# Scale of V in a windowed-attention and gated-MLP kernel: row sums transposed by a transfer instead of by TensorE

## The chip, the cores and the metric

The kernel runs on one core of a Trainium2 chip. The metric is the device time of one execution in microseconds (us); the kernel before has a median of 650.21 us in 3 runs (648.14 to 650.54). The engines are named as in the profile: PE (TensorE; its weight loads are listed apart as PEld), DVE (VectorE), ACT (ScalarE), POOL (GpSimd) and SP (SyncE, which issues the DMA transfers of this kernel). Each takes its instructions in order.

## The reference

Eight batches, each with 8 heads of 576 positions and 64 channels: attention with a window of 128 positions and a linear bias, then a gated MLP over the joined heads.

```python
scores = scale * np.matmul(q, k.transpose(0, 1, 3, 2))
mask = (rel >= 0) & (rel < window)                 # window = 128
scores = np.where(mask, scores + bias[None], -1000000000.0)
attn = np.exp(scores - np.max(scores, axis=-1, keepdims=True))
attn = attn / (np.sum(attn, axis=-1, keepdims=True) + 1e-09)
x = np.matmul(attn, v)                             # heads joined: (8, 576, 512)
...
h = np.maximum(x @ w_in, 0.0)                      # 512 -> 1024
u, v = (h[..., :d_ff // 2], h[..., d_ff // 2:])
v_n = (v - mu) / np.sqrt(var + 1e-06)
v_s = np.einsum('ts,bsd->btd', w_spatial, v_n) + b_spatial[None, :, None]
return ((u * v_s) @ w_out).astype(np.float32)
```

## The kernel before

Work is built from a planner. Each step is put in with `plan.add(engine, weight, due, f, reads, writes)`: an engine, an estimate of its time, a due time, and the parts of buffers that it reads and writes. `plan.order()` then walks through a modelled time and lets each engine take, of the steps whose inputs are there, the one that is due first; `plan.either` lets the engine that would be done first (ACT or DVE) have a step. The resulting order is what each engine's queue holds. A changed weight or a step left out can so move other steps, on every engine.

Attention goes by pairs of heads, 4 pairs in each of 8 batches. The first five pairs go another way (`raw_tile`). The other 27 go through `attention`, once each, and one such pass is called a unit here. In a unit, in the numbers of the lines of the kernel before:

- L409 and L411 load Q and K (`qkraw`) and V (`vraw`), three buffers each. L520 makes the scores on PE in two groups, into PSUM banks `s` (4 of them).
- L531 adds bias and mask and takes the maximum (DVE), L537 exponentiates and sums (ACT), L545 and L549 make the reciprocals (DVE).
- L557 (ACT) and L562 (DVE) write the scaled probabilities as two float16 parts, high and low, into `pq0` and `pq1`. L568 transposes each by one DMA transfer inside SBUF into `pt` (18 blocks of 128 columns).
- V is split in float16 parts as well, `vh` and `vl`, which needs a power of two that fits the largest V of the unit. L579 (ACT) takes absolute values and sums each of the 128 rows into `am`; the values go to `vl`, which is only scratch at that time. The largest of the 128 row sums, which lie on 128 partitions, is found with the help of PE: L583 transposes the column into one row of a PSUM bank `x`, L587 and L588 (DVE) take the maximum and clamp it as bfloat16, L593 spreads it to all partitions by two products with constant rows `ones` (2^-12 and 2^-13/4096), and L599 and L600 (DVE) keep the exponent bits: the scale for V in `am` column 5, the one for the result in column 6.
- L604 (DVE) or L607 (ACT) writes `vh`, L611 (DVE) `vl`. L624 multiplies probabilities and V on PE into two banks `x` (2 of them), L633 (ACT) and L637 (DVE) write the result's two parts to `xt`, half by half.

The MLP of a batch goes by units of 8 to 14 products into PSUM banks `m` (2 of them): L689 and L711 (columns that are normalised, 4 groups and 1 group), L741 (`u`), L762 (the product along the positions), L788 (output `o`, copied out of the bank at L267 by ACT or DVE and stored by L798). PE's queue interleaves the MLP of one batch with the attention of the next. The seam between two batches is where the last L788 of one is followed by the first L689 of the next, which needs `xt` of all four units.

Of the kernel before, what the change touches and what calls it, by code (L numbers as in the profile page):

```python
# [9 lines left out]
F32 = mybir.dt.float32  # L10
F32R = mybir.dt.float32r
BF16 = mybir.dt.bfloat16
# [126 lines left out]
def attn_gmlp_kernel(ctx, tc, qk, v, w_in, w_spT, b_sp, w_out, outT):  # L139
# [3 lines left out]
    nc = tc.nc  # L143
# [31 lines left out]
    def fixed(shape, dtype, name):  # L175
        t = const.tile(shape, dtype, name=name)
        return Buf(lambda: t)

    def dve(n, fast=False):
        return 75 + n / (1.92 if fast else 0.96)  # L180
# [13 lines left out]

    nhalf = fixed([P, 1], F32, "nhalf")
    ident = fixed([P, P], F32, "ident")
    ones = fixed([1, 2 * P], BF16, "ones")
    tabs = [fixed([P, 2 * P], BF16, f"tab{h}") for h in range(H)]
    win = fixed([P, NC_, 2, DF], F32R, "win")
    wout = fixed([P, ND, 2, DM], F32R, "wout")  # L200
# [23 lines left out]
    def constants():  # L224
        def f():
            nc.gpsimd.iota(relf(), [[-1, 2 * P]], base=P, channel_multiplier=1, allow_small_or_imprecise_dtypes=True)
        plan.add("POOL", 400, 0, f, (), [(relf, 0)])

        def f():
            nc.vector.memset(maskt(), 0.0)  # L230
        plan.add("DVE", dve(256), 0, f, (), [(maskt, 0)])

        def f():
            nc.gpsimd.affine_select(maskt(), maskt(), [[-1, 2 * P]], ALU.is_ge, MASKED, base=P, channel_multiplier=1)
            nc.gpsimd.affine_select(maskt(), maskt(), [[1, 2 * P]], ALU.is_ge, MASKED, base=-1, channel_multiplier=-1)
        plan.add("POOL", 800, 1, f, [(maskt, 0)], [(maskt, 0)])

        def f():
            nc.vector.memset(ident(), 1.0)
            nc.vector.memset(ones()[:, :P], 2.0 ** -12)  # L240
            nc.vector.memset(ones()[:, P:], 2.0 ** -13 / PSC)
            nc.vector.memset(nhalf(), -0.5)
            nc.vector.memset(rstat(), 1.0)
        plan.add("DVE", dve(400), 500, f, (), [(ident, 0), (ones, 0), (nhalf, 0)] + [(rstat, k) for k in range(8)])

        def f():
            nc.gpsimd.affine_select(ident(), ident(), [[-1, P]], ALU.is_ge, 0.0, base=0, channel_multiplier=1)
            nc.gpsimd.affine_select(ident(), ident(), [[1, P]], ALU.is_ge, 0.0, base=0, channel_multiplier=-1)
        plan.add("POOL", 600, 500, f, [(ident, 0)], [(ident, 0)])

        def f():
            nc.vector.tensor_scalar(minus(), ident(), -1.0, None, ALU.mult)
        plan.add("DVE", 150, 501, f, [(ident, 0)], [(minus, 0)])
        for j in range(2):
            def f(j=j):
                nc.vector.memset(stat[j](), 1.0)
            plan.add("DVE", dve(64), 600, f, (), [(stat[j], x) for x in range(99)])
        for h in range(H):
            def f(h=h):
                slope = 2.0 ** (-8.0 * (h + 1) / H)  # L260
                nc.vector.scalar_tensor_tensor(tabs[h](), relf(), -8.0 * slope, maskt(), ALU.mult, ALU.add)
            plan.add("DVE", dve(256), 1000 + h * 4000, f, [(relf, 0), (maskt, 0)], [(tabs[h], 0)])
# [237 lines left out]
    def attention(b, p):  # L500
# [70 lines left out]

        vh, vl = (plan.buf(work, tag, 2, [P, NQ, P], F16) for tag in ("vh", "vl"))
        am = plan.buf(work, "am", 2, [P, 8], F32)
        one = plan.buf(work, "one", 2, [1, 2], BF16)
        mp = plan.buf(ps, "x", 2, [P, 512], F32)
        d = due - 3000

        def f():
            nc.scalar.activation(vl(), vr(), AF.Abs, accum_out=am()[:, 0:1])  # L579
        plan.add("ACT", act(NQ * P, 1), d, f, VRS, [(vl, 0), (am, 0)])  # L580

        def f():
            nc.tensor.transpose(mp()[0:1, 0:P], am()[:, 0:1], ident())  # L583
        plan.add("PE", SWITCH // 2, d + 1, f, [(am, 0), (ident, 0)], [(mp, 0)])

        def f():
            nc.vector.tensor_reduce(one()[:, 0:1], mp()[0:1, 0:P], AX.X, ALU.max)  # L587
            nc.vector.tensor_scalar(one()[:, 0:1], one()[:, 0:1], 2.0 ** -98, 2.0 ** 126, ALU.max, ALU.min)  # L588
        plan.add("DVE", 400, d + 2, f, [(mp, 0)], [(one, 0)])

        def f():
            for k in range(2):
                nc.tensor.matmul(mp()[:, P + k:P + k + 1], ones()[:, k * P:(k + 1) * P], one()[:, 0:1], start=True, stop=True,  # L593
                                 skip_group_check=True)
        plan.add("PE", SWITCH, d + 3, f, [(one, 0), (ones, 0)], [(mp, 1)])

        def f():
            bits = 0x7F800000
            nc.vector.tensor_scalar(am()[:, 5:7].bitcast(I32), mp()[:, P:P + 2].bitcast(I32), bits, None, ALU.bitwise_and)  # L599
            nc.vector.tensor_scalar(am()[:, 5:6].bitcast(I32), am()[:, 5:6].bitcast(I32), bits, None, ALU.bitwise_xor)  # L600
        plan.add("DVE", 150, d + 4, f, [(mp, 1)], [(am, 1)])

        def fv():
            nc.vector.tensor_scalar(vh(), vr(), am()[:, 5:6], None, ALU.mult)  # L604
# [4 lines left out]

        def f():  # L610
            nc.vector.scalar_tensor_tensor(vl(), vr(), am()[:, 5:6], vh(), ALU.mult, ALU.subtract)  # L611
        plan.add("DVE", dve(NQ * P) + 30, d + 6, f, VRS + [(am, 1), (vh, 0)], [(vl, 0)])

        xt = plan.buf(work, "xt", 6, [P, 2 * S + R], F32R)
        xps = [plan.buf(ps, "x", 2, [P, 512], F32) for _ in range(2)]
# [257 lines left out]
```

## Time and profile before

| | |
|---|---|
| Median of 3 runs | 650.21 us (648.14 to 650.54) |
| Profiled execution | 648.05 us, span 646.3 us, granted clock 0.992 |
| Busy of PE, PEld, DVE, ACT, POOL | 96%, 82%, 81%, 67%, 5% of the span |
| Transpose L583 | 27 times, 270 ns |
| Spreading products L593 | 54 times, 158 ns |
| Transfers L568 | 54, 4.7 us from issue to landing (median) |

The span is the profiled execution without what lies before its first and after its last instruction. A share of the span is a mean over the beginning (weights are prepared, raw pairs), some six equal batches, and an end without attention. In the windows and the timeline the first number is the start in us from the span's start, the second the time.

### The profile page before, as it was taken

The page shows a single profiled execution, that of the slowest core. Times are in us where ns is not written, and L with a number is a line of the kernel's source. Part 1 is how long each engine was busy: PE and PEld are TensorE (multiplying, and loading weights), DVE is VectorE, ACT ScalarE, POOL GpSimd, SP SyncE. Part 2 cuts the span into 40 slices and gives each one's busy share as a digit, 9 for nine tenths or more (in the row PEclk, how much of TensorE's full clock was granted, in tenths as well). Part 3 has the DMA queues.
Part 4 walks back from the last instruction along what each step waited for, and adds up shares of the span by engine and source line. Part 5 has one row for each costly group of instructions (what it writes and reads, how often), then busy time and mean ns, then how long its engine had stood idle before and what let it go on. Part 6 is the DMA issues. An engine that isn't in the chain of part 4 may idle for free.

```text
span 646.3 us, 14141 instructions
## 1 busy us (share of the span) xinstructions
PE 619.0 (96%) x5037; PEld 529.8 (82%) x5037; DVE 524.2 (81%) x1897; ACT 430.9 (67%) x1322; POOL 29.6 (5%) x53
## 2 busy tenths in 40 slices
PE   4879999999999999999999999999999999999997
PEld 2445688778899879988898979988898978988997
DVE  6999898999887979887887979887887979873632
ACT  4698675989585848686686848676686857662211
POOL 1000010000200010000100010000100010000100
PEclk9998799999999999999999999999999999999999
DMA  7903013799156863778165753858166751733001
GB/s 264 329 20 130 19 62 119 169 209 202 55 132 133 190 107 93 155 155 184 40 143 127 191 112 89 154 152 188 32 154 125 193 113 10 132 79 76 2 20 55
DMA packets 149291, 79.34 MB, mean 123 GB/s; under 512 B 128610, under 2 KB 139874, under 8 KB 149220
## 3 DMA queue, kind: packets, MB, share of 16 engines
q1 hardware_dynamic: 149220, 78.44, 51.8%
q8 instruction: 39, 0.64, 0.4%
q14 instruction: 32, 0.26, 0.1%
HBM read 37.13 MB, written 9.44 MB: 72 GB/s over the span
## 4 chain that ended last, share of the span: by engine, by line
PE 79%; DVE 17%; issue 1%; DMA 1%; ACT 1%; SPq 1%; ACTq 0%; DVEq 0%
PE m L762 16%; PE m L741 16%; PE m L788 14%; PE m L689 13%; PE s L520 8%; PE x L624 6%; DVE pq L562 4%; PE m L711 2%; DVE prob L436 2%; DVE prob L531 2%; DVE gs L298 1%; DMA pt<-in_qk_dram 1%; DVE prob L450 1%; DVE u L770 1%; DVE o L267 1%
## 5 line engine op out<-in xcount | busy, mean ns | idle before, releaser
L537 ACT ACTIVATE prob<-prob,stat 128x128 f32<-128x128 f32 (+1 forms) x270 | 125.4, 466 | 13.6 <-DVE stat L531 12.4
L762 PE MATMUL m<-wsp,vn 128*128 128x288 f32 x768 | 124.3, 299 | 0.7 <-DVE u L770 0.7
L788 PE MATMUL m<-gs,wout 128*128 128x288 f32 x768 | 113.5, 301 | 0.3 <-DVE gs L776 0.2
L762 PEld LDWEIGHTS m<-wsp,vn 128*128 128x128 f32 x768 | 107.5, 188 | 6.7 <-issue 1.9
L557 ACT ACTIVATE pq<-prob,stat 128x128 f16<-128x128 f32 x270 | 103.1, 464 | 12.7 <-ACT prob L537 10.2
L741 PE MATMUL m<-xt,win 128*128 128x288 f32 x768 | 111.6, 298 | 0.0
L788 PEld LDWEIGHTS m<-gs,wout 128*128 128x128 f32 x768 | 103.3, 188 | 7.2 <-issue 1.7
L562 DVE SCALAR_TENSOR_TENSOR pq<-prob,stat,pq 128x128 f16<-128x128 f32 x270 | 104.0, 437 | 4.3 <-ACT pq L557 3.7
L741 PEld LDWEIGHTS m<-xt,win 128*128 128x128 f32 x768 | 103.9, 188 | 4.1 <-issue 2.3
L689 PE MATMUL m<-win,xt 128*128 128x512 f32 x384 | 93.5, 396 | 1.7 <-DVE o L267 1.7
L531 DVE CUSTOM_DVE_ANT_0 prob<-s,tab 128x128 f32<-128x128 f32 (+1 forms) x270 | 89.2, 376 | 2.6 <-PE s L520 2.1
L689 PEld LDWEIGHTS m<-win,xt 128*128 128x128 f32 x384 | 71.5, 189 | 18.2 <-DVE o L267 2.8
L520 PE MATMUL s<-qkraw 64*128 64x256 f32 (+2 forms) x540 | 66.5, 360 | 1.5 <-DVE stat L531 1.3
L770 DVE TENSOR_TENSOR u<-m,u 128x288 f32<-128x288 f32 x64 | 28.9, 451 | 34.2 <-PE m L762 34.2
L520 PEld LDWEIGHTS s<-qkraw 64*128 64x128 f32 (+1 forms) x540 | 42.0, 175 | 16.2 <-issue 9.0
L659 POOL TENSOR_TENSOR st<-st,nhalf 128x1 f32<-128x1 f32 (+1 forms) x40 | 25.6, 640 | 560.4 <-DVE st L655 548.0
L537 ACT ACTIVATION_READ_ACCUMULATOR prob<-prob,stat 128x1 f32 x270 | 50.6, 187 | 0.0
L267 ACT COPY o<-m 128x288 f32<-128x288 f32 x37 | 14.6, 395 | 46.2 <-PE m L788 45.9
L624 PE MATMUL x<-pt,vh 128*64 128x256 f16 (+6 forms) x756 | 41.7, 229 | 0.0
L271 ACT ACTIVATE vt<-m 128x512 f32<-128x512 f32 x31 | 18.5, 598 | 33.0 <-DVE st L654 16.1
L637 DVE SCALAR_TENSOR_TENSOR xt<-x,am,xt 128x288 fp32r<-128x288 f32 x54 | 26.2, 507 | 17.1 <-ACT xt L633 17.0
L624 PEld LDWEIGHTS <-vh 128*64 128x64 f16 x756 | 31.7, 110 | 5.8 <-issue 3.5
(132 smaller groups left out, 820.7 us busy)
## 6 DMA issues: line engine op xcount, KB each, us to landing
qkraw<-in_qk_dram SPq DMA_DIRECT2D x28, 576.0 KB, 3.9
out_dram<-o SPq DMA_DIRECT2D x64, 144.0 KB, 2.0
vraw<-in_v_dram SPq DMA_DIRECT2D x28, 320.0 KB, 2.9
vn<-in_w_in_dram SPq DMA_DIRECT2D x6, 512.0 KB, 7.1
pt<-in_w_out_dram SPq DMA_DIRECT2D x4, 512.0 KB, 4.5
gs<-in_w_spT_dram SPq DMA_DIRECT2D x4, 288.0 KB, 5.0
xt<-in_w_in_dram SPq DMA_DIRECT2D x2, 512.0 KB, 6.8
qkraw<-in_qk_dram SPq DMA_DIRECT2D x3, 320.0 KB, 8.3
```

The costliest lines, as they stand in the source:

```text
L520: nc.tensor.matmul(sc[k][j]()[:m, i, :k1 - k0], raw()[rows, 0, t * P:t * P + m], raw()[rows, 1, k0:k1], start=True, stop=True)
L531: nc.vector.tensor_tensor_reduce(pt(), sc()[:m, i, :n], tabs[h]()[:m, c0:c0 + n], -0.125, 3e38, ALU.add, ALU.min, st()[:m, NM, j, t:t + 1])
L537: nc.scalar.activation(pt(), pt(), AF.Exp, bias=st()[:m, NM, j, t:t + 1], scale=-1.0, accum_out=st()[:m, SM, j, t:t + 1])
L557: nc.scalar.activation(pq[j]()[:m, 0, cs], prob[j]()[:m, cs], AF.Copy, scale=st()[:m, RC, j, t:t + 1])
L562: nc.vector.scalar_tensor_tensor(pq[j]()[:m, 1, cs], prob[j]()[:m, cs], st()[:m, RC, j, t:t + 1], pq[j]()[:m, 0, cs], ALU.mult, ALU.subtract)
L624: nc.tensor.matmul(xp()[j * D:(j + 1) * D, x0:x0 + n], l()[:, kt, j * D:(j + 1) * D], rhs[:, o:o + n], start=j not in seen, stop=False, sk ...
L637: nc.vector.scalar_tensor_tensor(xt()[:, S + R + hf * HS:S + R + (hf + 1) * HS], xp()[:, :HS], am()[:, 6:7], xt()[:, qs].bitcast(F32), ALU ...
L689: nc.tensor.matmul(pt(), xt[c]()[:, X0[a] + t * P:X0[a] + (t + 1) * P], win()[:, c, w, DH:DF], start=(n == 0), stop=(n == 3 * NC_ - 1))
L741: nc.tensor.matmul(pt()[:, :HS], win()[:, c, w, d * P:(d + 1) * P], xt[c]()[:, X0[a] + hf * HS:X0[a] + (hf + 1) * HS], start=(n == 0), sto ...
L762: nc.tensor.matmul(pt()[:, :HS], l, r, start=(n == 0), stop=(n == len(ops) - 1))
L770: nc.vector.tensor_tensor(u(), pt()[:, :HS], u(), ALU.mult)
L788: nc.tensor.matmul(pt()[:, :HS], wout()[:, d, w, e * P:(e + 1) * P], gs[d]()[:, a, :], start=(n == 0), stop=(n == 3 * ND - 1))
```

## The change

Per unit, the column of row sums is copied 128 times side by side as bfloat16 into the first of the five 128-column blocks of `vl` (`wide(0)`, new L584, on DVE), and one DMA transfer from SP transposes this 128x128 block inside SBUF into the second block (`wide(1)`, new L588). Every partition then holds all 128 sums, and DVE does the rest there in one step of five instructions: maximum (new L593), clamp (L594), exponent bits (L595), product with the two constants in `powers`, which takes the place of `ones` (L596), and the inversion of the exponent for the scale of V (L597). The three instructions on PE, their bank `x` and the bfloat16 buffer `one` go. The planner is told 300 for the transfer and 600 for the step on DVE. Lines behind it lose 3 in number: L624 becomes L621, L689 L686, L788 L785.

```diff
-        one = plan.buf(work, "one", 2, [1, 2], BF16)
-        mp = plan.buf(ps, "x", 2, [P, 512], F32)
...
         def f():
             nc.scalar.activation(vl(), vr(), AF.Abs, accum_out=am()[:, 0:1])
-        plan.add("ACT", act(NQ * P, 1), d, f, VRS, [(vl, 0), (am, 0)])
-
-        def f():
-            nc.tensor.transpose(mp()[0:1, 0:P], am()[:, 0:1], ident())
-        plan.add("PE", SWITCH // 2, d + 1, f, [(am, 0), (ident, 0)], [(mp, 0)])
-
-        def f():
-            nc.vector.tensor_reduce(one()[:, 0:1], mp()[0:1, 0:P], AX.X, ALU.max)
-            nc.vector.tensor_scalar(one()[:, 0:1], one()[:, 0:1], 2.0 ** -98, 2.0 ** 126, ALU.max, ALU.min)
-        plan.add("DVE", 400, d + 2, f, [(mp, 0)], [(one, 0)])
-
-        def f():
-            for k in range(2):
-                nc.tensor.matmul(mp()[:, P + k:P + k + 1], ones()[:, k * P:(k + 1) * P], one()[:, 0:1], start=True, stop=True,
-                                 skip_group_check=True)
-        plan.add("PE", SWITCH, d + 3, f, [(one, 0), (ones, 0)], [(mp, 1)])
+        plan.add("ACT", act(NQ * P, 1), d, f, VRS, [(vl, 0), (vl, 1), (am, 0)])
+
+        wide = lambda k: vl()[:, k, :].bitcast(BF16)
+
+        def f():
+            nc.vector.tensor_copy(wide(0), am()[:, 0:1].to_broadcast([P, P]))
+        plan.add("DVE", dve(P), d + 1, f, [(am, 0)], [(vl, 0)])
+
+        def f():
+            nc.sync.dma_start_transpose(out=wide(1), in_=wide(0))
+        plan.add("SP", 300, d + 2, f, [(vl, 0)], [(vl, 1)])
 
         def f():
             bits = 0x7F800000
-            nc.vector.tensor_scalar(am()[:, 5:7].bitcast(I32), mp()[:, P:P + 2].bitcast(I32), bits, None, ALU.bitwise_and)
+            nc.vector.tensor_reduce(am()[:, 1:2], wide(1), AX.X, ALU.max)
+            nc.vector.tensor_scalar(am()[:, 2:3], am()[:, 1:2], 2.0 ** -98, 2.0 ** 126, ALU.max, ALU.min)
+            nc.vector.tensor_scalar(am()[:, 2:3].bitcast(I32), am()[:, 2:3].bitcast(I32), bits, None, ALU.bitwise_and)
+            nc.vector.tensor_scalar(am()[:, 5:7], powers(), am()[:, 2:3], None, ALU.mult)
             nc.vector.tensor_scalar(am()[:, 5:6].bitcast(I32), am()[:, 5:6].bitcast(I32), bits, None, ALU.bitwise_xor)
-        plan.add("DVE", 150, d + 4, f, [(mp, 1)], [(am, 1)])
+        plan.add("DVE", 600, d + 4, f, [(vl, 0), (vl, 1), (powers, 0)], [(am, 1)])
```

What this does to the order, at three places of a steady batch. First PE in the middle of a batch, between two output units (`m<-gs,wout`) and the product along the positions (`m<-wsp,vn`); the last two rows of the piece of before come twice there.

```order
L788 MATMUL m<-gs,wout 128x288 x12
L583 MATMUL x<-ident,am 1x128
L520 MATMUL s<-qkraw 64x192 x2
L788 MATMUL m<-gs,wout 128x288 x12
L593 LDWEIGHTS ones
L593 MATMUL x<-one,ones 128x1
```

The same place in the changed kernel:

```order
L785 MATMUL m<-gs,wout 128x288 x12
L520 MATMUL s<-qkraw 64x192 x2
L785 MATMUL m<-gs,wout 128x288 x12
L759 MATMUL m<-wsp,vn_3078 128x288 x3
L759 MATMUL m<-r_80,l_3120 128x288
```

The transpose and the spreading products are gone, and the large products follow each other. Second PE at the seam, before; the L593 rows come twice again, and L624 of the next batch's first unit follows.

```order
L788 MATMUL m<-gs,wout 128x288 x24
L583 MATMUL x<-ident,am 1x128
L689 MATMUL m<-win,xt 128x512 x12
L593 LDWEIGHTS ones
L593 MATMUL x<-one,ones 128x1
```

And after:

```order
L621 MATMUL x<-pt,vl 64x64
L785 MATMUL m<-gs,wout 128x288 x12
L686 MATMUL m<-win,xt 128x512 x12
L708 MATMUL m<-win,xt 128x512 x8
L686 MATMUL m<-win,xt 128x512 x36
L621 LDWEIGHTS vh
```

The last unit's product with V (L621) has moved one output unit closer to the seam, and that of the next batch's first unit stands behind all four groups of L686 and directly ahead of an L520 (before it stood after two of them). The last unit's L621 likewise follows an L520 directly. Third SP around one new transfer, at the seam (buffer numbers are kept here; o is an output block), before:

```order
L568 DMA_TRANSPOSE pt_5095<-pq0_85 128x18x128
L798 DMA out_0_dram<-o_5119 128x288
L568 DMA_TRANSPOSE pt_5130<-pq1_86 128x18x128
L798 DMA out_0_dram<-o_5145 128x288
L411 DMA vraw_5188<-in_v_dram 128x640
L409 DMA qkraw_5394<-in_qk_dram 128x1152
```

And after:

```order
L568 DMA_TRANSPOSE pt_5115<-pq0_85 128x18x128
L568 DMA_TRANSPOSE pt_5156<-pq1_86 128x18x128
L588 DMA_TRANSPOSE vl_5132<-vl_5132 128x128
L411 DMA vraw_5291<-in_v_dram 128x640
L409 DMA qkraw_5367<-in_qk_dram 128x1152
```

The new transfer stands behind the two large transposes of another unit, at this place and at one more of the four in a batch; at the other two it has a load or a store ahead of it. On DVE 14 to 22 instructions stand between the copy (L584) and the maximum (L593) that reads the transfer's result; at the place where the transfer follows the two large ones in the middle of a batch they are 15, at the seam 14. Over the whole program 10 of the 19 steps that write `vh` on DVE move to ACT.

More of the change, by code (lines that the diff above doesn't have):

```diff
@@ L196, in attn_gmlp_kernel @@
     ident = fixed([P, P], F32, "ident")
-    ones = fixed([1, 2 * P], BF16, "ones")
+    powers = fixed([P, 2], F32, "powers")
     tabs = [fixed([P, 2 * P], BF16, f"tab{h}") for h in range(H)]
@@ L239, in f @@
             nc.vector.memset(ident(), 1.0)
-            nc.vector.memset(ones()[:, :P], 2.0 ** -12)
-            nc.vector.memset(ones()[:, P:], 2.0 ** -13 / PSC)
+            nc.vector.memset(powers()[:, 0:1], 2.0 ** -12)
+            nc.vector.memset(powers()[:, 1:2], 2.0 ** -13 / PSC)
             nc.vector.memset(nhalf(), -0.5)
             nc.vector.memset(rstat(), 1.0)
-        plan.add("DVE", dve(400), 500, f, (), [(ident, 0), (ones, 0), (nhalf, 0)] + [(rstat, k) for k in range(8)])
+        plan.add("DVE", dve(400), 500, f, (), [(ident, 0), (powers, 0), (nhalf, 0)] + [(rstat, k) for k in range(8)])
         def f():
@@ L611, in f @@
             nc.vector.scalar_tensor_tensor(vl(), vr(), am()[:, 5:6], vh(), ALU.mult, ALU.subtract)
-        plan.add("DVE", dve(NQ * P) + 30, d + 6, f, VRS + [(am, 1), (vh, 0)], [(vl, 0)])
+        plan.add("DVE", dve(NQ * P) + 30, d + 6, f, VRS + [(am, 1), (vh, 0)], [(vl, 0), (vl, 1)])
         xt = plan.buf(work, "xt", 6, [P, 2 * S + R], F32R)
```

## The prediction

> **What bounds the kernel now.** I read the head of the page first, then the chain that ended last, in order of time, and last one steady stretch in the table of windows. The first group of L689 opens a batch; it starts at 299.65 and again at 372.61, so one batch takes 72.96 us, and that is the window.
>
> ```profile
> span 646.3 us, 14141 instructions
> PE 619.0 (96%) x5037; PEld 529.8 (82%) x5037; DVE 524.2 (81%) x1897; ACT 430.9 (67%) x1322; POOL 29.6 (5%) x53
> 299.65 3.03 PE m L689 x12
> 372.61 3.03 PE m L689 x12
> core 0: us, PE busy (x) PEld busy (x) DVE busy (x) ACT busy (x) POOL busy (x), PEclk, DMA share, GB/s
> 299.65:372.61 72.96, 72.53 (x620) 63.58 (x620) 61.04 (x224) 52.12 (x164) 3.17 (x5) 1.00 0.57 133
> ```
>
> PE is busy for 72.53 of 72.96 us at the full granted clock. So PE's stream of instructions sets the length of a batch, and what is taken out of that stream comes off the time, unless another engine makes PE wait. DVE has 72.96 - 61.04 = 11.9 us of idle time per batch, ACT 20.8. That is the reserve into which the change may push work.
>
> **The PE work that goes.** Each of 27 attention units loses a transpose (L583) and two one-column products (L593). Their durations are one price; what stands around them in PE's own order of time is the other, because matmuls overlap.
>
> ```profile
> L583 PE MATMUL x<-ident,am x27: 270/271/276, 110.2 to 571.6; 128*1 128x128 f32 x27
> L593 PE MATMUL x<-one,ones x54: 158/159/173, 112.5 to 574.1; 1*128 1x1 bf16 x54
> 203.68 3.44 PE L788 MATMUL m<-gs,wout 128*128 128x288 f32 x24
> 206.96 0.28 PE L583 MATMUL x<-ident,am 128*1 128x128 f32 x1
> 207.16 0.54 PE L520 MATMUL s<-qkraw 64*64 64x192 f32 x4
> 207.63 1.85 PE L788 MATMUL m<-gs,wout 128*128 128x288 f32 x12
> 209.42 0.20 PE L593 MATMUL x<-one,ones 1*128 1x1 bf16 x2
> 209.55 0.67 PE L762 MATMUL m<-wsp,vn 128*128 128x288 f32 x3
> 226.68 0.28 PE L583 MATMUL x<-ident,am 128*1 128x128 f32 x1
> 226.71 3.01 PE L689 MATMUL m<-win,xt 128*128 128x512 f32 x12
> 229.65 0.20 PE L593 MATMUL x<-one,ones 1*128 1x1 bf16 x2
> 229.78 2.11 PE L711 MATMUL m<-win,xt 128*128 128x512 f32 x8
> 236.07 5.77 PE L689 MATMUL m<-win,xt 128*128 128x512 f32 x24
> 241.77 1.79 PE L520 MATMUL s<-qkraw 64*128 64x128 f32 x16
> ```
>
> Starts give the price in place. The 24 products from 203.68 to the start of L583 at 206.96 take 3.28, or 1.64 for 12; the 12 from 207.63 to the next real work at 209.55 take 1.92, with L593 inside: 0.28 for L593. L583 holds the stream from 206.96 to 207.16: 0.20. That unit pays 0.48. The other: 24 L689 take 241.77 - 236.07 = 5.70, or 2.85 for 12; with L593 behind them 229.78 - 226.71 = 3.07, so 0.22; and L583 ahead of that group began only 0.03 before it (226.68), so 0.25. The mean of 0.48 and 0.25 is 0.37, and 27 x 0.37 = 9.9 us. The two ends are 27 x 0.25 = 6.7 and 27 x 0.48 = 13.0.
>
> Waits belong to it as well. PE's weight loads wait before L593 and L583:
>
> ```profile
> PEld L593 <- issue: 7.0, 27, 0.9
>   DVE xt L637: 2.2, 8
>   DVE one L588: 0.9, 1
> PE m L689 <- DVE o L267: 1.7, 4, 0.4
> ```
>
> The 7.0 us of "issue" is inside the 0.22 to 0.28 already. The 2.2 (L583 waiting for a free x bank) and 0.9 go with their instructions, but weight loads wait partly in the shade of the product before: 0.9 to 3.1, I take 1.5. The last row is another wait at the seam between batches: the first L689 needs an m bank that DVE's copy of o frees, 1.7 us of PE in 4 batches, 0.43 each. In the new order DVE makes that copy before it turns to most of the L562 of that unit, and two L520 and the L624 lie between; I count 1.0 as gained, from 0 to 1.7.
>
> **What the new order does to PE.** Without the small steps the planner puts L624 next to L520 at two places of each batch, where before both stood alone between groups of L689, L741 or L788. Each visit to another kind of product costs an issue wait going in and one coming out:
>
> ```profile
> 241.77 1.39 PEld L520 LDWEIGHTS s<-qkraw 64*128 64x128 f32 x16 [0.36 <-issue]
> 243.49 1.63 PEld L741 LDWEIGHTS m<-xt,win 128*128 128x128 f32 x12 [0.33 <-issue]
> ```
>
> A merged visit saves one such pair at most, 0.69 us, of which the products still in the array hide a part: 0 to 0.69, times 2, times 6 batches, is 0 to 8.3. I take 0.17 each, so 2.0: the low end, since the engine's row shows only 0.43 us without a product in the whole batch.
>
> At two other places cover is lost. The L624 of a batch's last unit had two output units (L788) behind it and now has one; and in the last batch it has none, so L689 follows at once.
>
> ```profile
> 580.83 5.50 PE L788 MATMUL m<-gs,wout 128*128 128x288 f32 x36
> 587.77 1.87 PE L788 MATMUL m<-gs,wout 128*128 128x288 f32 x12
> 587.65 0.52 DVE L637 SCALAR_TENSOR_TENSOR xt<-x,am,xt 128x288 fp32r<-128x288 f32 x1 [4.94 <-ACT xt L633]
> ```
>
> L624 ends about when the next unit starts, 587.77, and the first half of xt is done at 587.65 + 0.52 = 588.17; with a unit of 1.7 us behind it that hides, with nothing it is about 0.6 us of waiting (0.4 to 1.5, if L711 too waits for the second half). So once +0.6, and nothing in the other batches while the unit hides it; without that cover it would be 0.6 in each of six, 3.6.
>
> **The work that comes.** DVE, per unit:
>
> ```profile
> L587 DVE TENSOR_REDUCE one<-x 1x1 bf16<-1x128 f32 x27 | 7.4, 273 | 0.0
> L588 DVE TENSOR_SCALAR one<-one x27: 144/144/146, 111.7 to 572.5; 1x1 bf16<-1x1 bf16 x27
> L599 DVE TENSOR_SCALAR am<-x 128x2 int32<-128x2 int32 x27 | 4.1, 154 | 12.3 <-PE x L593 12.3
> L600 DVE TENSOR_SCALAR am<-am 128x1 int32<-128x1 int32 x27 | 4.2, 154 | 0.9
> L267 DVE CAST gs<-u 128x288 fp32r<-128x288 f32 x38 | 11.6, 306 | 0.5
> L267 DVE CAST xt<-xt 128x64 fp32r<-128x64 f32 x5 | 0.9, 189 | 0.1
> L604 DVE TENSOR_SCALAR vh<-vraw,am 128x640 f16<-128x640 f32 x19 | 10.5, 551 | 0.2
> ```
>
> Out go 273 + 144 + 154 + 154 = 725 ns. In come the copy to 128 columns (between 189 and 306; I take 225), the maximum (273), and four small operations (144 + 3 x 154 = 606): 1104. That is +0.38 a unit, +1.5 a batch. Ten vh move from DVE to ACT (-5.5 us in all), some copies come the other way. DVE so goes from 61.0 to about 62 of some 71 us: 9 us of reserve stay. ACT gets those ten vh over the whole run, little beside its 20.8 us of idle time per batch. The work itself costs the path nothing; its cover is PE's stream.
>
> The wait is the question. L593 of the new kernel (the maximum) stands in DVE's queue behind a transfer, and all of softmax and the copies that free PE's m banks are queued behind it.
>
> ```profile
> DVE u L770 <- PE m L762: 34.2, 27, 6.9
> pt<-pq SPq DMA_TRANSPOSE x54, 4.7
> L568 SPq DMA_TRANSPOSE pt<-pq x54: 2399/2725/3772, 118.7 to 580.7; - x54
> out_dram<-o SPq DMA_DIRECT2D x64, 144.0 KB, 2.0
> ```
>
> No small transpose inside SBUF is in the trace. It lands after 2.0 us at the low end (the store of o, the shortest transfer) and 4.7 at the high one (a transpose with 18 times the columns); I take 2.5, near the low end, because its data are 32 KB. Its issue is short if it goes by columns: 2.73/18 = 0.15. Between the copy and the maximum the order has 14 to 22 DVE instructions; at 61.04/224 = 0.27 us each that is 3.8 to 6.0 us before DVE can get there. So alone the transfer is hidden. At two of a batch's four places it stands on SP right behind the two big ones of another unit, which start when DVE has finished that unit's pq: 2 x 2.73 + 2.5 = 8.0 us against the 4.1 of 15 instructions there, a wait of up to 3.9 if DVE runs without a stop, and none if DVE has to wait for the L762 and L520 in between, as it did in the trace (34.2 us for L762 in all). I take 0.4 us of PE a batch for it, 2.5 in all, between 0 and 13. What stands on SP behind the new transfer (loads of V, Q and K, stores of o) has room: PE's whole time without a product in the steady window is 0.43 us, so no load is late there.
>
> The Trainium skill (VectorE: DVE Perf Modes, "Rules for kernel authors" and "The three transpose paths") speaks against this change: transpose 128x128 on TensorE if PSUM will do, since it takes 390 ns there and 1309 ns by DMA. The trace has 271 ns for TensorE, less than the page. By the page's figures, as an estimate, each scale comes about 0.9 us later and the forecast stays, since the order leaves more room than that.
>
> **The sum.** -9.9 (products) - 1.5 (their waits) - 1.0 (seam) - 2.0 (merged visits) + 0.6 (last batch) + 2.5 (DVE waiting for the transfer) = -11.3 us. The profiled run took 648.05, 1.7 more than its span, and is 2.2 below the median of 650.21, so I put the change on the median: 638.9, rounded to 639.
>
> **Rivals.** (1) The products were hidden anyway: PE's 96% is a modelled figure, and L583 began only 0.03 us before the next group at 226.71. Then only the low price counts and the merged visits give nothing: -6.7 - 0.9 + 0.6 + 2.5 = -4.5, 646. Against it: the wait of issue at each of the 27. (2) Slower: the transfer lands late on DVE. It decides when DVE's reserve of 9 us a batch is used up, at four waits of 2.3 us; each further microsecond goes to PE. At waits of 3.0 that is 4 x 0.7 = 2.8 a batch, 19 over 27/4 batches, against the 13.8 that the other terms gain: 655. At the 3.9 worked out above it is 679. For it: DVE has no other queue; against it: 14 to 22 instructions of distance. The page named above would have it so, since by its rule the transpose belongs on PE. (3) The new order feeds PE worse: the L520 of two units now stand with one L741 group between them, and DVE must empty four score banks in time. A wait of 1.5 us in each of six batches, 9 us, leaves 648. (4) The order does better: the visits at their full 8.3: 633.
>
> **How the numbers follow.** Under 0.5% (3.3 us) this kernel's runs can't be told apart. Forecast 0.60 (634 to 645), rival 1 0.10, rival 3 0.12, rival 2 0.12, rival 4 0.06. Faster, below 647: the forecast, rival 4, most of rival 1 and a part of 3, 0.76; same 0.11; slower, rival 2 and little else, 0.13. The range from 633 to 649 takes in rivals 1, 3 and 4 and leaves out rival 2 and some tails.
>
> **What would show it.** Right: a batch (L689 to L686 in the new numbers) of about 71.3 us instead of 72.96, PE still without gaps, the new DMA landing in 2 to 3 us, and DVE's L593 with little idle time before it. Wrong: idle time on DVE before L593 released by the DMA, PE waiting for DVE on m or s banks, a batch above 72.5, or a long issue of the small transpose on SP. Most likely to break it: a small transpose that is not small for the DMA queue.

## The result, and the profile after

The changed kernel takes 646.88 us (median of 8 runs, 643.62 to 647.96) against 650.39 for the kernel before on the same chip (8 runs). The ratio is 0.9949, 95% interval 0.9927 to 0.9971: a gain of 0.5%, 3.3 us on 650, where 11.3 were forecast. The time lies inside the range of 633 to 649, but the gain is less than a third of the forecast.

The profiled execution of the changed kernel is the longest of its 8 (647.96 us), that of the kernel before one of the shortest (648.05). Their spans are equal by accident, so the traces are compared batch by batch. The head of the page of the changed kernel:

```profile
span 646.3 us, 14066 instructions
PE 613.9 (95%) x4956; PEld 530.3 (82%) x4956; DVE 536.8 (83%) x1955; ACT 434.0 (67%) x1318; POOL 30.0 (5%) x53
PEclk9998799897999999999999999999999999999999
```

PE works 5.1 us less (619.0 before), DVE 12.6 us more (524.2 before). In the clock row two more slices than before fall below 9 tenths, the 8th and the 10th (each is 16 us): here the first attention batch stands.

A batch is now measured from the start of its `v_rem` group (L711 before, L708 after: the products of the rest columns) to the next one's, because that group has the same neighbours in all orders. In the table of windows (length, then busy time of PE, PEld, DVE, ACT and POOL, granted clock, DMA share, GB/s) these are the first attention batch of the kernel before; then of the changed kernel the first attention batch, the fourth batch and the sixth:

```profile
85.95:159.19 73.24, 70.53 (x616) 61.17 (x614) 67.56 (x257) 59.23 (x191) 2.52 (x4) 1.00 0.67 147
...
86.50:164.57 78.07, 71.71 (x587) 62.68 (x586) 68.12 (x253) 57.86 (x182) 2.53 (x4) 0.93 0.57 133
308.11:380.46 72.35, 71.03 (x609) 62.86 (x608) 64.46 (x238) 53.23 (x165) 3.29 (x5) 1.00 0.62 137
451.70:522.94 71.24, 70.69 (x610) 62.95 (x608) 63.36 (x235) 52.16 (x162) 3.29 (x5) 1.00 0.61 138
```

The sixth batch takes 71.24 us, where 71.3 were forecast. But the first attention batch is 4.8 us longer than before (78.07 against 73.24), with 6.36 us in which PE has no product (2.71 before) and a mean granted clock of 0.93, and the third and fourth batches take 72.4. In the first attention batch DVE was busy for 67.56 of 73.24 us before, 92%; the prediction worked with a steady batch alone.

What PE waits for, in the view of waits (engine and line, releaser: total us, times, longest), and in the timeline the longest of the four stops of the first row and the one right behind it, where the bracket is the idle time before:

```profile
PE s L520 <- DVE stat L531: 5.9, 4, 3.2
PE m L759 <- DVE u L272: 1.8, 6, 0.3
PE m L759 <- DVE u L767: 1.1, 6, 0.2
...
124.43 0.88 PE L520 MATMUL s<-qkraw 64*64 64x192 f32 x4 [3.17 <-DVE stat L531]
125.80 0.44 PE L520 MATMUL s<-qkraw 64*128 64x128 f32 x1 [0.50 <-DVE stat L531]
```

Before, the first of these rows was this:

```profile
PE s L520 <- DVE stat L531: 1.3, 2, 0.8
```

The other two stops of that row, 0.86 and 1.34 us, stand before 148.48 and 150.35 in the same batch. So PE, which lost its small products, now waits for DVE at the score banks, in the first attention batch alone. The new transfer itself, in the views of DMA issues, of instructions (ns: least, median, most) and of waits:

```profile
vl<-vl SPq DMA_TRANSPOSE x27, 3.1
L588 SPq DMA_TRANSPOSE vl<-vl x27: 1112/1173/2189, 109.8 to 564.9; - x27
DVE am L593 <- DMA vl<-vl: 1.2, 1, 1.2
```

It is not small for the queue (1.17 us of issue, 3.1 us to landing), yet DVE waited for it once in 27 times.

### The profile page after: what moved, and what is told of

The parts are those of the page before. It is cut to its first block, busy times and chain, and to the rows that moved or that the text cites. A ratio compares the mean times of both kernels' runs of the same rounds, so it can differ in the third digit from the quotient of the medians.

```text
span 646.3 us, 14066 instructions
## 1 busy us (share of the span) xinstructions
PE 613.9 (95%) x4956; PEld 530.3 (82%) x4956; DVE 536.8 (83%) x1955; ACT 434.0 (67%) x1318; POOL 30.0 (5%) x53
## 5 line engine op out<-in xcount | busy, mean ns | idle before, releaser
L785 PE MATMUL m<-gs,wout 128*128 128x288 f32 x768 | 116.3, 305 | 0.8 <-DVE u L767 0.4
L785 PEld LDWEIGHTS m<-gs,wout 128*128 128x128 f32 x768 | 106.0, 192 | 9.7 <-DVE stat L531 2.0
L557 ACT ACTIVATE pq<-prob,stat 128x128 f16<-128x128 f32 x270 | 104.5, 465 | 10.5 <-DVE stat L545 5.4
L562 DVE SCALAR_TENSOR_TENSOR pq<-prob,stat,pq 128x128 f16<-128x128 f32 x270 | 106.0, 434 | 4.4 <-ACT pq L557 3.3
L531 DVE CUSTOM_DVE_ANT_0 prob<-s,tab 128x128 f32<-128x128 f32 (+1 forms) x270 | 90.1, 375 | 13.8 <-PE s L520 12.6
L686 PE MATMUL m<-win,xt 128*128 128x512 f32 x384 | 92.5, 396 | 1.2 <-DVE o L267 1.0
L686 PEld LDWEIGHTS m<-win,xt 128*128 128x128 f32 x384 | 72.8, 191 | 17.7 <-DVE o L267 1.2
L520 PE MATMUL s<-qkraw 64*128 64x256 f32 (+2 forms) x540 | 66.1, 367 | 5.9 <-DVE stat L531 5.9
L520 PEld LDWEIGHTS s<-qkraw 64*128 64x128 f32 (+1 forms) x540 | 42.1, 179 | 17.5 <-DVE stat L531 7.3
L267 ACT COPY o<-m 128x288 f32<-128x288 f32 x32 | 12.7, 396 | 49.9 <-PE m L785 47.0
L621 PE MATMUL x<-pt,vh 128*64 128x256 f16 (+6 forms) x756 | 41.7, 229 | 0.0
L621 PEld LDWEIGHTS <-vh 128*64 128x64 f16 x756 | 31.7, 110 | 6.2 <-issue 6.2
L621 PE MATMUL x<-pt,vl 128*64 128x256 f16 (+6 forms) x378 | 35.3, 228 | 0.0
L647 DVE BATCH_NORM_STATS2 st<-vt 128x6 f32<-128x512 f32 (+1 forms) x40 | 27.4, 686 | 7.7 <-ACT vt L271 7.5
```

The lines of the kernel that those rows point to most:

```text
L520: nc.tensor.matmul(sc[k][j]()[:m, i, :k1 - k0], raw()[rows, 0, t * P:t * P + m], raw()[rows, 1, k0:k1], start=True, stop=True)
L531: nc.vector.tensor_tensor_reduce(pt(), sc()[:m, i, :n], tabs[h]()[:m, c0:c0 + n], -0.125, 3e38, ALU.add, ALU.min, st()[:m, NM, j, t:t + 1])
L557: nc.scalar.activation(pq[j]()[:m, 0, cs], prob[j]()[:m, cs], AF.Copy, scale=st()[:m, RC, j, t:t + 1])
L562: nc.vector.scalar_tensor_tensor(pq[j]()[:m, 1, cs], prob[j]()[:m, cs], st()[:m, RC, j, t:t + 1], pq[j]()[:m, 0, cs], ALU.mult, ALU.subtract)
L621: nc.tensor.matmul(xp()[j * D:(j + 1) * D, x0:x0 + n], l()[:, kt, j * D:(j + 1) * D], rhs[:, o:o + n], start=j not in seen, stop=False, sk ...
L647: nc.vector.bn_stats(st()[:m, 0:6], vt()[:m])
```

## The experiments

Theory 1: the PE products were worth what was forecast, and the missing part was lost to the added DVE work, above all in the first attention batch, where DVE was already nearly full. Theory 2: the new order that the planner writes makes the waits by itself. Theory 3: the stretches at half clock come by chance. Each ratio is against the kernel before on the same chip, with a 95% interval; us in brackets are the ratio's difference from 1 on 650.

### 1. Old order, no work for the scale

```diff
-            nc.tensor.transpose(mp()[0:1, 0:P], am()[:, 0:1], ident())
+            pass
...
-            nc.vector.tensor_scalar(vh(), vr(), am()[:, 5:6], None, ALU.mult)
+            nc.vector.tensor_scalar(vh(), vr(), powers()[:, 0:1], None, ALU.mult)
```

> The kernel before, instruction order kept, but the scale of V is not computed: the tiny PE transposes and products and the small DVE steps between them are left out and constant powers of two stand in (row sums by ScalarE's Abs stay). It prices the 27 units' PE products alone, with nothing put in their place. The prediction's terms for that are 9.9 + 1.5 + 1.0 us, so about 637.5 on 650 (bounds 633 to 641). Theory 1 (the products were worth what was forecast; the missing part was lost to the work that was added) expects 636 to 641, with the first attention batch no longer than before (73.2 us between its first v_rem groups and the next batch's) and steady batches of 71.0 to 71.5. The rival (the products were partly hidden, so the forecast's first term was too large) expects 644 to 648.

Measured: 639.33 us, ratio 0.9856 (0.9834 to 0.9878; -9.4 us). A steady batch in the kernel before; then, in this one, the first attention batch and a steady one:

```profile
448.67:521.64 72.97, 72.54 (x622) 63.58 (x621) 61.05 (x223) 52.15 (x164) 3.17 (x5) 1.00 0.59 133
...
87.24:159.75 72.51, 70.61 (x603) 61.42 (x602) 65.95 (x242) 59.64 (x193) 2.52 (x4) 0.98 0.65 147
443.46:514.99 71.53, 71.01 (x609) 63.07 (x608) 59.00 (x207) 51.98 (x163) 3.17 (x5) 1.00 0.61 135
```

The run gains 9.4 us (7.9 to 10.8). With the products it loses DVE's four old steps too, 0.73 us a unit, so the gain need not be PE's alone; in a steady batch it is. PE's busy time falls by 1.53 us there, 0.38 for each of four units, and its idle time does not fall (0.43, now 0.52). So the products were not hidden, and the old DVE steps cost PE nothing there that shows. The forecast had 0.37 a unit, 9.9 in all, and 1.5 for their waits; its 1.0 at the seam doesn't come with this order, where PE still waits for DVE's copy of `o`.

### 2. New order, no work for the scale

The changed kernel with the bodies of the copy, the transfer and the five steps replaced by `pass` and the same constants. PE's order is that of the changed kernel row for row.

> The changed kernel, instruction order kept, but the scale of V is not computed: DVE's copy, the small transfer and DVE's five steps are left out and constant powers of two stand in. It prices the added work at the new order. Theory 1 (added DVE work and transfer in a batch in which DVE is full) expects the 3.2 us PE gap and the half-clock stretch of the first attention batch to go, that batch to be at most 73 us instead of 78.1, and a time of 636 to 641. Theory 2 (the order that the planner now writes makes the hole by itself: score groups of two units close together while DVE has yet to empty the banks) expects the gap and the half clock to stay, that batch above 76 us, and 643 to 646. Theory 3 (half-clock stretches come by chance) expects them to differ between runs whatever is left out.

Measured: 635.73 us, ratio 0.9802 (0.9776 to 0.9827; -12.9 us). The first attention batch, and a steady one:

```profile
87.36:162.18 74.82, 71.35 (x588) 62.94 (x587) 64.34 (x228) 57.34 (x182) 2.52 (x4) 0.93 0.60 139
442.95:513.00 70.05, 70.05 (x610) 62.92 (x609) 59.76 (x210) 52.01 (x162) 3.28 (x5) 1.00 0.62 138
```

The order alone gains 3.5 us more than the first run (1.3 to 5.7 by the two intervals), and a steady batch has no gap left on PE. From here to the changed kernel the added work takes 9.6 us back. Both theories have a share, though: the hole at the score banks, as PE's stops there are called from here on, is there without any added work (3.3 us in 2 waits, the longest 2.0; 5.9 in 4 in the changed kernel), and with it the half clock. By the order alone the first attention batch is 2.3 us longer than in experiment 1 (74.82 against 72.51), while a steady one is 1.5 shorter. That part of theory 1's expectation, that the hole would go, was wrong.

### 3. Old order, new work

Copy and transfer are written behind ScalarE's Abs step, the five steps in the place of DVE's two mask steps.

```diff
             nc.scalar.activation(vl(), vr(), AF.Abs, accum_out=am()[:, 0:1])
+            nc.vector.tensor_copy(wide(0), am()[:, 0:1].to_broadcast([P, P]))
+            nc.sync.dma_start_transpose(out=wide(1), in_=wide(0))
```

> The old order of instructions, the new way of the scale: PE's tiny products are out; DVE's copy and SP's small transfer are written right behind ScalarE's Abs step, and DVE's five steps where DVE's old mask step stood, 1 to 26 DVE rows behind the copy. It has all the added work and none of the new order. Theory 1 (added work) expects a longer first attention batch again (76 us or more) and a time of 644 to 650; DVE now also waits for the transfer in units whose distance is short, up to 3 us each, which could bring it above 650. Theory 2 (new order) expects no hole in the first attention batch and about 639 to 642, unless DVE's waits for the transfer show as PE waits, which the chain of waits would tell.

Measured: 656.1 us, ratio 1.0115 (1.0093 to 1.0138). This run has a fault of its own. DVE's copy, right behind ScalarE's step, made DVE stand:

```profile
DVE vl L584 <- ACT vl L583: 17.2, 24, 1.0
```

It never waited for the transfer. Its direction speaks for theory 1; its size says nothing, and experiment 12 puts the question cleanly.

### 4. The first attention batch the old way

```diff
+        if b == 1:
+            one = plan.buf(work, "one", 2, [1, 2], BF16)
+            mp = plan.buf(ps, "x", 2, [P, 512], F32)
...
+        else:
+            wide = lambda k: vl()[:, k, :].bitcast(BF16)
```

> The changed kernel with the three units of the first attention batch alone made the old way (tiny PE products, no transfer); the other 24 units go the new way. Theory 1 (the added DVE work in that one batch costs PE 3.6 us of waits and half-clock stretches of about 5 us) expects the batch back at about 73.2 us, less one half-clock pair, and a time of 640 to 642. Theory 2 (the new order, which stays nearly the same in that batch) expects 645 to 647 with the batch at 76 us or more. Theory 3 (chance) expects the same as the changed kernel, 643 to 648.

Measured: 641.28 us, ratio 0.9887 (0.9867 to 0.9908; -7.3 us). The first attention batch:

```profile
87.01:161.50 74.49, 71.80 (x613) 62.55 (x611) 67.42 (x255) 58.02 (x187) 2.52 (x4) 0.98 0.65 143
```

Three of 27 units give back 4.0 of the 9.6 us, and their batch 3.6 (78.07 to 74.49; PE's time without a product 6.36 to 2.69). The time is the one that theory 1 named, but the run does not decide between the theories: in this batch PE's order is again that of the kernel before, group by group, so order, products and DVE work change together. Without any added work the new order gave this batch 74.82 us (experiment 2).

### 5 and 6. Transfer alone, five steps alone

Both are experiment 2 with one part put back: the copy and the transfer; or the five steps on a constant table.

```diff
+            nc.vector.tensor_reduce(am()[:, 1:2], tabs[0]()[:, :P], AX.X, ALU.max)
...
```

> The changed kernel in its own order with DVE's copy and SP's small transfer kept and DVE's five steps behind it left out (constant powers of two stand in for the scale of V, so nothing waits for the transfer but the later users of the vl buffer). It splits the 1.5% (9.6 us) between the new order without scale work and the changed kernel. If the price is DVE's time (theory 1: 0.21 us of 1.17 us a unit is the copy), it is 637 to 639 and the first attention batch keeps a gap near 2 us. If it is the transfer (its 1.17 us of issue on SP's queue, what stands behind it there, its 3.1 us of landing), it is 642 to 646, with stores of o late at the seams as in the changed kernel.

> The other half: the changed kernel in its own order with DVE's five steps kept, run on a constant table, and the copy and the transfer left out (constant powers of two are used as the scale). DVE never waits here for a transfer and SP has no extra row. Theory 1 (price is DVE's time, 0.96 us of 1.17 us a unit) expects 641 to 645, with PE waits for DVE of about 1 us in a steady batch and a first attention batch of 76 us or more. If the price is the transfer, it is 636 to 638 with a first batch of about 75 us.

Measured: with copy and transfer 635.45 us, ratio 0.9788 (0.9765 to 0.9811), the same as without them and less than the 637 to 639 expected for the copy's time on DVE. With the five steps 645.5 us, ratio 0.9925 (0.9912 to 0.9939): +8.0 us on experiment 2 (6.1 to 9.9). The five steps carry the price, copy and transfer alone none that shows. In the waits of the run with the five steps alone, and in its steady batch, stand nearly the rows of the changed kernel; the row that starts at 87.22 is its first attention batch:

```profile
PE s L520 <- DVE stat L531: 4.9, 3, 2.7
PE m L759 <- DVE u L272: 1.7, 6, 0.3
...
87.22:163.43 76.21, 71.14 (x587) 62.66 (x586) 67.22 (x248) 57.56 (x182) 2.52 (x4) 0.93 0.57 135
450.71:521.95 71.24, 70.69 (x609) 62.98 (x608) 62.87 (x231) 51.96 (x163) 3.29 (x5) 1.00 0.60 136
```

Its steady batch is 1.2 us longer than in experiment 2, for 3.1 us more of DVE (62.87 against 59.76). Of the 1.2 us, 0.55 are idle time of PE; by the other 0.64 the same products keep PE busy for longer (70.69 against 70.05), which no run here takes apart. The first attention batch is 1.4 us longer than in experiment 2 (76.21 against 74.82), so of the 8.0 us most lies in the other batches; theory 1's "above all in the first attention batch" does not hold for the five steps. In the changed kernel, with copy and transfer, that batch takes another 1.9 us (78.07); in experiment 5, with these two alone, it takes 73.35, less than without them. Each of these is one profiled execution, and the half clock in this batch differs between them, so the parts of this one batch are not settled. In the changed kernel DVE waits up to 2.6 us at a seam for a store of `o`; the transfer on SP's queue is not the cause, since that wait is here too (2.7).

### 7. Is half clock a consequence of idle time?

The kernel before with four more clamps between L588 and L593, in the first attention batch only.

```diff
+            for _ in range(4 if b == 1 else 0):
+                nc.vector.tensor_scalar(one()[:, 0:1], one()[:, 0:1], 2.0 ** -98, 2.0 ** 126, ALU.max, ALU.min)
```

> The kernel before with four more copies of its 0.144 us clamp step on DVE (0.58 us) between the two small PE steps of the three units in the first attention batch only; results unchanged. In the kernel before PE idles 0.33 and 0.90 us there, 1.23 us within one 3.41 us stretch of the clock's record, and the clock stays full; in the other kernels stretches with 1.27 us and more were followed by half clock. If a stretch with that much idle time does halve the clock of the next one, this kernel has 0.58 us of direct delay at one place (up to 1.7 if all three units show it) and 1.7 us for each half-clock stretch that the kernel before did not have: 650.5 to 653, and nearly all runs in that range. If half-clock stretches come by chance, it is 648.2 to 649.9 with as many of them as before.

Measured: 652.08 us (651.42 to 653.31), ratio 1.0035 (1.0024 to 1.0047; +2.3 us). Windows of 3.41 us in the kernel before (two), then in this one (two), at the place of the delay:

```profile
141.92:145.33 3.41, 2.18 (x17) 1.72 (x15) 3.38 (x14) 2.90 (x11) 0.00 (x0) 1.00 0.99 163
145.33:148.74 3.41, 3.36 (x24) 2.83 (x23) 3.38 (x17) 3.41 (x11) 0.00 (x0) 1.00 1.12 199
...
145.60:149.01 3.41, 1.97 (x12) 1.32 (x12) 3.21 (x18) 2.56 (x8) 0.00 (x0) 1.00 0.92 173
149.01:152.42 3.41, 3.41 (x16) 3.41 (x15) 3.06 (x14) 3.04 (x12) 0.00 (x0) 0.50 0.82 217
```

With PE idle for 1.23 us of a stretch (3.41 - 2.18) the next one was at full clock; with 1.44 at half. Between the two traces the batch grows from 73.24 to 76.86 us: 1.79 of waiting and 1.7 for the half of 3.41 us that was lost; the median over all runs grows by 2.3. This speaks against theory 3. So do the five profiled kernels that share the changed kernel's order on PE (it and experiments 2, 5, 6 and 9): half clock begins at 123.5 to 126.0 us in each.

### 9. Four steps instead of five

The clamp is folded into the copy, which runs on GpSimd; PE's and ScalarE's order stays that of the changed kernel.

```diff
-            nc.vector.tensor_copy(wide(0), am()[:, 0:1].to_broadcast([P, P]))
+            nc.gpsimd.tensor_scalar(wide(0), am()[:, 0:1].to_broadcast([P, P]), 2.0 ** -98, 2.0 ** 126, ALU.max, ALU.min)
...
-            nc.vector.tensor_scalar(am()[:, 2:3], am()[:, 1:2], 2.0 ** -98, 2.0 ** 126, ALU.max, ALU.min)
```

> The changed kernel with PE's and ScalarE's order unchanged row for row; the clamp is folded into the copy, the copy runs on GpSimd at the same place of the program, and DVE keeps four of its steps. Nothing is left out of the computation. Added DVE time per unit is about 0.81 us, against 0 in the run without scale work (ratio 0.980), 0.96 in the run with five steps alone (0.9925) and 1.17 in the changed kernel (0.9949). If the price goes with DVE's time, about 1.3% per 0.96 us, the ratio is 0.990 to 0.992 (643 to 644.5 on 649.5) and the hole of the first attention batch about 2.5 us. If it is a fixed price of any steps at that place, the ratio stays at 0.992 to 0.995.

Measured: 643.65 us, ratio 0.9896 (0.9879 to 0.9912), at the cheap edge of what was expected (0.990 to 0.992), with a steady batch of 70.64 us instead of 71.24. The hole was expected to shrink to 2.5 us and stayed at 3.04: it is no plain function of DVE's time.

### 10. One number of the planner

```diff
-        plan.add("DVE", 600, d + 4, f, [(vl, 0), (vl, 1), (powers, 0)], [(am, 1)])
+        plan.add("DVE", 1000, d + 4, f, [(vl, 0), (vl, 1), (powers, 0)], [(am, 1)])
```

> The changed kernel with one number changed: the planner's cost of DVE's five steps is 1000 ns instead of 600 (measured: 0.96 us). The same work; the planner should give ScalarE more of the copies that either engine can make, and spread the steps. If the loss comes from a DVE that the planner believes emptier than it is, the time is 639 to 644; if the hole of the first attention batch comes from the order of the score groups whatever the planner believes, 644 to 648.

Measured: 640.48 us, ratio 0.9851 (0.9836 to 0.9866; -9.7 us), 6.4 us better than the changed kernel with the same work. The engines' row, a steady batch and the first attention batch:

```profile
PE 610.3 (96%) x4956; PEld 527.7 (83%) x4956; DVE 529.4 (83%) x1942; ACT 443.2 (69%) x1331; POOL 27.6 (4%) x53
...
445.86:516.20 70.34, 70.34 (x610) 62.80 (x608) 62.47 (x232) 53.94 (x164) 2.81 (x5) 1.00 0.63 139
85.97:162.22 76.25, 70.96 (x587) 61.97 (x586) 66.70 (x252) 58.41 (x183) 2.52 (x4) 0.96 0.62 143
```

DVE gave 7.4 us of work away and ScalarE took 9.2; in the steady batch PE waits for nothing, with DVE 62.47 us busy, hardly less than the 62.87 of experiment 6. So it is not the amount of DVE work alone that makes PE wait in a steady batch, but what stands where in the queues, which the planner wrote anew on all engines. The first attention batch is still 76.25.

### 8 and 11. A version faster than both

Experiment 4 together with the four steps of 9 (8), and the same with the planner told 850 for the four steps (11).

> A version meant to be faster than both: first attention batch the old way as in the run before of that kind; in the others the clamp is folded into the copy, the copy runs on GpSimd (5% busy) and DVE keeps four steps (0.28 + 0.15 + 0.23 + 0.15 = 0.81 us a unit instead of 1.17). If DVE's time is the price (theory 1), the 1.2 us of PE waits in each steady batch shrink to about 0.8 and it takes 638.5 to 640.5 against 641.3. If GpSimd's copy is slow enough to bring the transfer late onto DVE, 641 to 645.

> The version meant to be fastest (first attention batch the old way, four DVE steps, copy on GpSimd; ratio 0.980) with the planner's cost of the four steps at 850 ns instead of 600 (measured about 0.8 us). If the planner's belief matters, ScalarE takes more copies and it is 634 to 636.5 on 650; if not, 636 to 639.

Measured: 636.98 us, ratio 0.9799 (0.9786 to 0.9812), and 637.44 us, ratio 0.9808 (0.9786 to 0.9830): 2% faster than the kernel before, 1.5% than the changed one. In 8 the first attention batch is as before the change, at full clock, and a steady batch has 0.28 us of waits:

```profile
86.21:159.47 73.26, 70.36 (x612) 61.06 (x611) 67.88 (x259) 58.66 (x191) 4.66 (x6) 1.00 0.63 146
440.70:511.34 70.64, 70.36 (x610) 62.96 (x608) 62.37 (x227) 51.45 (x162) 6.07 (x9) 1.00 0.63 139
```

8 came out 1.5 us below the lower edge of what was expected (638.5). The planner's order changed too; that this is the reason is not shown. A number nearer to the measured cost, which gained 1% in 10, gained nothing in 11.

### 12. Old order, five steps alone

Experiment 1 with the five steps on the constant table, in the place of DVE's two mask steps.

> The kernel before in its own order without PE's small products (as in the first run of this study: ratio 0.9856), with DVE's five steps run on a constant table where DVE's two mask steps stood; copy and transfer left out, constant powers of two as the scale. With the run that has the five steps alone in the new order (0.9925 against 0.9802 without them, so 1.25% for the steps) it makes a square of order and steps. If the price of the steps does not hang on the new order, the ratio is 0.995 to 1.001 (1.0% to 1.5% over 0.9856). If the new order is what makes them dear, it is 0.986 to 0.990. The run with copy and transfer in the old order (1.0115) had DVE standing 17.2 us for ScalarE's Abs step, so its size says little.

Measured: 646.87 us, ratio 0.9953 (0.9938 to 0.9969): +6.3 us on experiment 1 (4.6 to 8.1). The square of order and steps, as ratios:

| | no scale work | five steps alone | the whole new way |
|---|---|---|---|
| old order | 0.9856 | 0.9953 | 1.0115 (see 3) |
| new order | 0.9802 | 0.9925 | 0.9949 (the changed kernel) |

The steps cost 6.3 us in the old order and 8.0 in the new; the difference is within the intervals. So the new order is better at either side of the square, and theory 2, that it made the loss, falls for the run as a whole. What stays of it is the first attention batch, where the order by itself makes stops of 2.0 and 1.3 us and costs 2.3 us.

## Why the prediction was wrong

**The products** (9.9 and their waits 1.5): 9.4 us measured with DVE's old steps, 7.9 to 10.8. The price from two places in the stream of starts held (0.38 us of PE a unit against 0.37), and rival 1 is refuted. The waits added little to it.

**The order** (seam 1.0, merged visits 2.0, last batch -0.6): 3.5 us measured together, between experiments 1 and 2, where 2.4 were forecast. That the total comes near is luck. In a steady batch the order is worth 1.48 us (71.53 to 70.05 between these runs), three times the 0.5 that seam and merged visits come to when spread over six batches; in the first attention batch it costs 2.3, which had no term in the sum.

**DVE waiting for the small transfer** (2.5): once, for 1.2 us, and copy and transfer alone cost nothing that was measured (experiment 5). Its parts were mis-sized and it didn't matter: 1.17 us of issue instead of 0.15, a landing of 3.1 instead of 2.5. So the issue does not go by columns alone. Between the five steps alone and the changed kernel lie 1.6 us (0.9925 to 0.9949), which is this transfer and the copy together and no more than the intervals allow.

**DVE's added work, the step that failed**: "The work itself costs the path nothing; its cover is PE's stream." The sum has nothing for it. The five steps cost 8.0 us in the new order (6.1 to 9.9), 6.3 in the old. These are the rows of the five steps and the copy in the changed kernel (busy us, mean ns of one):

```profile
L593 DVE TENSOR_REDUCE am<-vl 128x1 f32<-128x128 bf16 x27 | 7.4, 275 | 1.2 <-DMA vl<-vl 1.2
L594 DVE TENSOR_SCALAR am<-am 128x1 f32<-128x1 f32 x27 | 4.1, 154 | 0.9
L595 DVE TENSOR_SCALAR am<-am 128x1 int32<-128x1 int32 x27 | 4.1, 153 | 0.9
L596 DVE TENSOR_SCALAR am<-powers,am 128x2 f32<-128x2 f32 x27 | 6.2, 229 | 1.0
L597 DVE TENSOR_SCALAR am<-am 128x1 int32<-128x1 int32 x27 | 4.2, 154 | 0.9
L584 DVE CAST vl<-am 128x128 bf16<-128x128 f32 x27 | 6.2, 233 | 0.7
```

The sizes were nearly right (1.20 us a unit with the copy, 1.10 forecast), though DVE's busy time in a steady batch went from 61.05 to 63.36 us and not to about 62, as other copies came over from ScalarE for the ten `vh`. Wrong was to set the work against DVE's idle time of 9 us in a batch. DVE takes its instructions in order, so idle time elsewhere is no cover here. DVE's rows at one of the stops of a steady batch, and then the product on PE that stops:

```profile
402.71 1.85 DVE L562 SCALAR_TENSOR_TENSOR pq<-prob,stat,pq 128x256 f16<-128x256 f32 x5
404.49 0.44 DVE L272 TENSOR_SCALAR u<-m 128x288 f32<-128x288 f32 x1
...
404.98 0.66 PE L759 MATMUL m<-wsp,vn 128*128 128x288 f32 x3 [0.31 <-DVE u L272]
```

The copy that frees PE's bank (L272) stands behind five L562; in experiment 2, with the same order but for the added rows, PE has no such stop. In this batch DVE is idle for 7.8 of 71.24 us, but for only 0.3 of the last 3.7 ahead of that product. Experiment 3 shows the same from the other side: one instruction that had to wait made DVE stand for 17.2 us in all, with its other work behind it. And not every batch is like the window that was read: in the first attention batch, DVE's 67.56 of 73.24 us left 5.7, not 11.9.

**The net.** -9.4 (products) - 3.5 (order) + 8.0 (five steps) + 1.6 (the rest) = -3.3 us, the measured change; as each term is the step from one run to the next, they add up to it by construction. The steady batch hit its forecast (71.24 against 71.3) only because two errors met: products and order took 2.9 us out of it (72.97 to 70.05 in experiment 2), not 1.7, and DVE's steps put 1.2 back. That, too, was luck.

**Rival 3** named the right mechanism and place, L520 waiting for DVE to empty the score banks of two units, but six times 1.5 us in steady batches; it came in the first attention batch alone, and dearer, since half clock follows. **Rival 2** is refuted as a wait for the transfer; as a price of DVE's time it came before the reserve was used up. **Rival 4**, 633, comes near what order and products give together without the added work (635.7), but it counted on the merged visits alone.

What stays open: which part of the hole of the first attention batch a better order would remove. Experiment 10 shortened it without clearing it, 4 and 8 avoided it. How the new steps' price divides among the waits was not taken apart, nor what DVE's four old steps cost at their place outside the steady batches: whatever that is stands in the 9.4 us of the products. A third buffer for `o`, against the late stores at the seams, wasn't tried.

## What to carry to other kernels

Work added to an in-order engine is not covered by that engine's idle time in a batch: look at what stands behind it in its queue and who waits for that, in the fullest stretch of the run as well as in the steadiest one. It is worth trying to give a planner the measured cost of a new step: told 1000 ns instead of 600 for one of 965, it wrote an order 1% faster, though in another version the same gained nothing. And when PE is 96% busy, a microsecond of waiting that falls together with others can be charged twice, by the wait and by the clock.

## What the runs showed of the hardware

The granted clock of TensorE goes by stretches of 3.41 us and multiples. In the attention batches of the 14 profiled kernels, each stretch of 3.41 us at full clock in which PE was idle for 1.44 us or more was followed by half clock for 3.41 or 6.83 us, and none with 1.24 or less was. In between both happened: half clock followed on 1.27 (experiment 4) and 1.29 (2), full clock on 1.29 (5 and 12) and 1.31 (the changed kernel). The idle time need not be in one piece. In the changed kernel (a stretch and what followed, twice):

```profile
122.57:125.98 3.41, 1.06 (x5) 0.56 (x6) 3.41 (x17) 2.90 (x13) 0.00 (x0) 1.00 0.94 171
125.98:129.39 3.41, 3.41 (x16) 2.45 (x16) 3.02 (x15) 3.14 (x14) 0.00 (x0) 0.50 1.04 177
146.46:149.87 3.41, 1.70 (x11) 1.11 (x9) 3.38 (x12) 2.58 (x8) 0.00 (x0) 1.00 1.16 159
149.87:156.70 6.83, 6.35 (x25) 5.81 (x26) 4.17 (x23) 5.55 (x21) 0.00 (x0) 0.50 0.65 185
```

Here 2.35 and 1.71 us without a product were followed by 10.24 us at half clock. The kernel before stood at 1.23, just below. During the preparation of the weights, with its other kinds of products, the sum of idle time does not separate the two as cleanly. The Trainium skill ("TensorE: Matmul & The Clock Gate", section "What's actually happening") has a free-running window of 3413 ns, and the traces agree with that length (3.41 us). The same page, under "Why this matters for your kernels", asks only that no gap be longer than about 3 us; here gaps that added up to 1.44 us in one window were enough.

A transpose of 128x128 in bfloat16 inside SBUF held SP's queue for 1.17 us at the median, 43% of what 18 such blocks take there (2.73), so by these two figures a large part of its issue does not grow with the number of blocks.
